# Turning q and k of two blocks in the two row halves of TensorE, in a kernel of gated attention and an FFN

## The chip, the cores and the metric

The kernel runs on one core of a Trainium2 chip. The metric is the device time of that core in microseconds (us). A core has a matrix engine (TensorE, in profiles PE, with its weight loads listed apart as PEld), a vector engine (DVE), a scalar engine (ACT), GpSimd (POOL), and a queue (SP) from which this kernel issues its DMA transfers. Matmuls read SBUF and write PSUM, which has eight banks of 512 fp32 values in each of 128 partitions; DVE and ACT read the results there.

## What is computed

A gated linear recurrence over 768 steps, for 4 batches of 8 heads with 48 channels, and a feed-forward network (FFN) on its output:

```python
# q, k, v, alpha: (4, 8, 768, 48); alpha in [0.8, 1.0)
for t in range(S):
    state = alpha[:, :, t, :, None] * state + np.einsum('bhd,bhe->bhde', k[:, :, t], v[:, :, t])
    y[:, :, t] = np.einsum('bhd,bhde->bhe', q[:, :, t], state)
# (B, H, S, D) -> (B*S, H*D) = (3072, 384)
x = y.transpose(0, 2, 1, 3).reshape(B * S, H * D)
h = np.maximum(x @ w_in, 0.0)      # w_in (384, 2048)
out = h * h @ w_out                # w_out (2048, 384)
```

The kernel computes the recurrence in 24 blocks of 128 tokens (6 stretches of each of 4 batches), with all 8 heads of a block in one tile. With b the running product of alpha within the block (the exponential of a cumulative sum of logarithms), q is multiplied by b and k by 1/b. The scores of a block are then a matmul of k and q, masked to the causal part, and the state enters and leaves a block through small matmuls. Matmuls contract over partitions, so for the scores q and k, which are loaded with a token in each partition, have to be turned: channels into partitions. TensorE does this with transposes against an identity matrix.

## The kernel before

Blocks come in groups of four (GB = 4). Group 0 runs first, in a fixed order; its FFN follows, with the attention of group 1 woven between its matmuls, and so on: while group g goes through its FFN, group g + 1 goes through its attention, in pairs of blocks. `PLAN` gives the places of a pair's steps in units of the FFN work; 20 blocks in 10 pairs are handled in this way. The heads are padded to 64 channels in the tiles of q and k, so that 128 columns hold two heads (a pair p of heads; NP = 4).

```python
    def kept(name, n, shape):
        return [consts.tile(shape, FP32, name=f"{name}{i}") for i in range(n)]
    s_t = [p2.tile([128, NP, 64], FP32, tag="s", name="s", bufs=B + 2) for _ in range(B)]
    for t in s_t:
        nc.gpsimd.memset(t, 0.0)
    NV = 4
    tiles = {
        "a": kept("a_in", 2, [128, H * D]), "q": kept("q_in", 2, [128, H, 64]),
        "k": kept("k_in", 3, [128, H, 64]), "v": kept("v_in", NV, [128, H * D]),
    }
    # ... cut ...
    def load(n, xs="aqkv"):
        c, b = divmod(n, B)
        for x in xs:
            t = tile_of(x, n)
            t = t[:, :, 0:D] if x in "qk" else t.rearrange("a (h d) -> a h d", h=H)
            src = srcs[x][b, :, c * C : (c + 1) * C, :].rearrange("h s d -> s h d")
            step = H // 2 if n == 0 and x in "ak" else H
            for h in range(0, H, step):
                nc.sync.dma_start(out=t[:, h : h + step], in_=src[:, h : h + step])
    # ... cut ...
    for n, xs in ((0, "akq"), (1, "aqk")):
        load(n, xs)
    # ... cut ...
    def warm(_):
        nc.tensor.matmul(
            out=ps_att.tile([128, NP, 64], FP32, tag="att", name="warm"),
            lhsT=s_t[0].rearrange("a p d -> a (p d)")[:, 0:128], rhs=s_t[0], start=True, stop=True,
        )
    # ... cut ...
    def bank(n, name, shape=(NP, C)):
        if n < GB and name in ("sc", "y"):
            return ps_ffn.tile([128, *shape], FP32, tag="f", name=name)
        return ps_att.tile([128, *shape], FP32, tag="att", name=name)
    # ... cut ...
    def ln(n):
        la = blk[n]["la"] = tile_of("a", n)
        for c in parts(n):
            nc.scalar.activation(out=la[:, c], in_=la[:, c], func=AF.Ln)
    def parts(n):
        return [slice(0, H * D)] if n else [slice(i * DM // 2, (i + 1) * DM // 2) for i in range(2)]
    def cs(n):
        ps = blk[n]["cs"] = bank(n, "cs")
        la = blk[n].pop("la")
        for c in parts(n):
            nc.tensor.matmul(
                out=ps.rearrange("a p t -> a (p t)")[:, c], lhsT=causal, rhs=la[:, c],
                start=True, stop=True, skip_group_check=True,
            )
    def sums_of_logs(n):
        return blk[n]["cs"].rearrange("a p t -> a (p t)")[:, 0 : H * D]
    def eb(n):
        b = blk[n]["b"] = p2.tile([128, H * D], FP32, tag="b", name="b")
        nc.scalar.activation(out=b, in_=sums_of_logs(n), func=AF.Exp)
    def ei(n):
        inv = blk[n]["inv"] = p2.tile([128, H * D], FP32, tag="inv", name="inv")
        for c in parts(n):
            nc.scalar.activation(
                out=inv[:, c], in_=sums_of_logs(n)[:, c], func=AF.Exp, scale=-1.0
            )
    def scaled(x, n, factor):
        for c in parts(n) if x == "k" else [slice(0, H * D)]:
            t = tile_of(x, n)[:, c.start // D : c.stop // D, 0:D]
            nc.vector.tensor_tensor(
                out=t, in0=t, in1=factor[:, c].rearrange("a (h d) -> a h d", d=D), op=ALU.mult
            )
    # ... cut ...
    def turned(x, n):
        rows = tile_of(x, n).rearrange("a h d -> a (h d)")
        ps = blk[n][f"{x}T"] = bank(n, f"{x}T")
        for p in range(NP):
            nc.tensor.transpose(
                out=ps[:, p, :], in_=rows[:, 128 * p : 128 * (p + 1)], identity=ident
            )
    def qT(n):
        turned("q", n)
    def kT(n):
        turned("k", n)
    VECTOR = ("k1", "k2", )
    def copied(x, n):
        t = blk[n][f"{x}s"] = work(f"{x}s", 2 if x == "k" else 4)
        copy = nc.vector.tensor_copy if f"{x}{n}" in VECTOR else nc.scalar.copy
        copy(out=t, in_=blk[n].pop(f"{x}T"))
    def qc(n):
        copied("q", n)
    def kc(n):
        copied("k", n)
    # ... cut ...
    HALF = [slice(0, 64), slice(64, C)]
    two = {}
    def scores(n):
        ps = two[n] = [bank(n, "sckv", (2, NP, 64)) for _ in range(2)]
        ks, qs = blk[n]["ks"], blk[n]["qs"]
        for p in range(NP):
            for h in range(2):
                for e in range(2):
                    rows = slice(64 * e, 64 * e + D)
                    nc.tensor.matmul(
                        out=ps[e][HALF[h], 0, p, :], lhsT=ks[rows, p, HALF[h]],
                        rhs=qs[rows, p, HALF[h]], start=True, stop=True, skip_group_check=True,
                    )
    # ... cut ...
    def state_sums(n):
        ps = two[n]
        for p in range(NP):
            for e in range(2):
                first = (2 * p + e) * D - G * e
                for h in range(1 if n // B == NCH - 1 else 2):
                    nc.tensor.matmul(
                        out=ps[h][64 * e : 64 * (e + 1), 1, p, :],
                        lhsT=tile_of("k", n)[HALF[h], 2 * p + e, :],
                        rhs=tiles["v"][n % NV][HALF[h], first : first + 64],
                        start=True, stop=True, skip_group_check=True,
                    )
    # ... cut ...
    def ga(a, n):
        if n is not None:
            for f in (scores, state_sums, masked, sums_copied):
                f(n)
        if a is not None:
            product = y_begin(a)
            for h in range(2):
                for m, p, e in heads(a):
                    rows = slice(64 * e, 64 * e + D)
                    s = blk[m]["u" if h else "s"]
                    product(m, p, e, s[rows, p, 0 : D + G * e], blk[m]["qs"][rows, p, HALF[h]], HALF[h])
            for m, p, e in heads(a):
                end = inner(product, m, p, e, e)
    # ... cut: the rest of ga, and gb, which does the same for block n + 1, then ev(a) copies y out of PSUM ...
    first = """
        warm0 ln0 load0v cs0 ei0 eb0 mk0 mq0 load2a load2q load2k bl0 ln1 kT0 qT0 kc0
        load1v qc0 cs1 load3a sc0 load3k eb1 mq1 bl1 qT1 load2v ei1 mk1 weights0 kT1 kc1
        ...
    """
    PLAN = (
        (0, "ln0"),
        (0.5, "ln1"),
        (2.0, "cs0 eb0 ei0"),
        (3.0, "cs1 eb1 ei1"),
        (3.5, "mk0"),
        (4.0, "bl0"),
        (4.5, "mq0 mk1 bl1"),
        (5.0, "mq1"),
        (6.5, "qT0 qc0 qT1 qc1 kT1 br1"),
        (7.5, "kc1"),
        (8.0, "kT0 kc0 br0"),
        (9.5, "ga"),
        (10.5, "gb"),
    )
```

`turned` is called four times for a pair of blocks (q and k of each): each call does four full 128x128 transposes into one PSUM bank, and `copied` brings the bank to SBUF with one copy. `ps_att` has four banks, which all steps of the attention share in turn; `ps_ffn` has the other four. The scores and state sums use quarters of the array (64 rows by 64 columns), with the two halves of the tokens in different quarters. `parts` and the step in `load` treat the first block by halves of its heads.

Of the kernel before, what the change touches and what calls it, by code (L numbers as in the profile page):

```python
# [10 lines left out]
AF = mybir.ActivationFunctionType  # L11
ALU = mybir.AluOpType
# [3 lines left out]
GB = 4  # L16
# [7 lines left out]
def kernel(  # L24
# [25 lines left out]
    nc = tc.nc  # L50
    B, H, S, D = q.shape
    C = 128
    NCH = S // C
    NP = H // 2
    NBLK = B * NCH
    DM, DF = moe_w_in.shape
# [37 lines left out]
    def flat(t):  # L94
        return t.rearrange("a x y -> a (x y)")
# [4 lines left out]
    for x, n, i in (("q", 2, 6), ("q", 3, 7), ("k", 3, 5)):  # L100
        t = lent[x, n] = flat(w_out[i])[:, 0 : 64 * H].rearrange("a (h d) -> a h d", h=H)
        nc.gpsimd.memset(t[:, :, D:64], 0.0)

    def tile_of(x, n):
        return lent.get((x, n), tiles[x][n % len(tiles[x])])


    srcs = {"a": alpha, "q": q, "k": k, "v": v}

    def load(n, xs="aqkv"):  # L110
        c, b = divmod(n, B)
        for x in xs:
            t = tile_of(x, n)
            t = t[:, :, 0:D] if x in "qk" else t.rearrange("a (h d) -> a h d", h=H)
            src = srcs[x][b, :, c * C : (c + 1) * C, :].rearrange("h s d -> s h d")
            step = H // 2 if n == 0 and x in "ak" else H
            for h in range(0, H, step):
                nc.sync.dma_start(out=t[:, h : h + step], in_=src[:, h : h + step])

    raws = {}  # L120

# [56 lines left out]
        )  # L178
        nc.vector.tensor_tensor(out=w, in0=w, in1=power.bitcast(FP32), op=ALU.mult)

    for n, xs in ((0, "akq"), (1, "aqk")):
        load(n, xs)
    to_load = list(range(2 * NW))
    stage = [3]
# [18 lines left out]
    ident = consts.tile([128, 128], FP32, name="ident")  # L203
    make_identity(nc, ident)
    causal = consts.tile([128, C], FP32, name="causal")
    make_upper_triangular(nc, causal, 1.0, diag=True)
    halves_mask = consts.tile([128, C // 2], FP32, name="halves_mask")
    for i in range(2):
        rows = slice(64 * i, 64 * (i + 1))
# [20 lines left out]
    blk = [{} for _ in range(NBLK)]  # L230
    xT = {}
# [7 lines that stand above are left out]
    def work(name, bufs=1):  # L239
        return p2.tile([128, NP, C], FP32, tag=name, name=name, bufs=bufs)  # L240

    def ln(n):
        la = blk[n]["la"] = tile_of("a", n)
        for c in parts(n):
            nc.scalar.activation(out=la[:, c], in_=la[:, c], func=AF.Ln)

    def parts(n):

        return [slice(0, H * D)] if n else [slice(i * DM // 2, (i + 1) * DM // 2) for i in range(2)]

    def cs(n):

        ps = blk[n]["cs"] = bank(n, "cs")
        la = blk[n].pop("la")
        for c in parts(n):
            nc.tensor.matmul(  # L256
                out=ps.rearrange("a p t -> a (p t)")[:, c], lhsT=causal, rhs=la[:, c],
                start=True, stop=True, skip_group_check=True,
            )

    def sums_of_logs(n):
        return blk[n]["cs"].rearrange("a p t -> a (p t)")[:, 0 : H * D]
# [4 lines left out]

    def ei(n):
        inv = blk[n]["inv"] = p2.tile([128, H * D], FP32, tag="inv", name="inv")
        for c in parts(n):  # L270
            nc.scalar.activation(
                out=inv[:, c], in_=sums_of_logs(n)[:, c], func=AF.Exp, scale=-1.0
            )

    def scaled(x, n, factor):
        for c in parts(n) if x == "k" else [slice(0, H * D)]:
            t = tile_of(x, n)[:, c.start // D : c.stop // D, 0:D]
            nc.vector.tensor_tensor(
                out=t, in0=t, in1=factor[:, c].rearrange("a (h d) -> a h d", d=D), op=ALU.mult
            )  # L280

    def mq(n):
        scaled("q", n, blk[n]["b"])
# [32 lines left out]
# [3 lines that stand above are left out]
        copy(out=t, in_=blk[n].pop(f"{x}T"))  # L319

    def qc(n):
        copied("q", n)

    def kc(n):
        copied("k", n)


    def zeros(n):
# [77 lines left out]
    HALF = [slice(0, 64), slice(64, C)]  # L406
# [57 lines left out]
    def dep(later, earlier):  # L464
        tc.add_manual_dep(
            later.ins, earlier.ins.name,
            mybir.DependencyInfo(mybir.DependencyClass.Sync, mybir.DependencyReason.DATA),
            reason="rows of TensorE change banks",
        )

    def inner(product, m, p, e, h):
        head = 2 * p + e
        return product(
            m, p, e, tiles["v"][m % NV][HALF[h], head * D - G * e : (head + 1) * D],
            am_h(m)[HALF[h], e, m % 2, p, :], HALF[h],
        )

    def heads(a):
        return [(m, p, e) for m in (a, a + 1) for p in range(NP) for e in range(2)]
# [23 lines left out]
    def gb(a, n):  # L503

        if a is not None:
            product, passed = two.pop("y")
            for i, (m, p, e) in enumerate(heads(a)):
                begin = inner(product, m, p, e, 1 - e)
                if i == 0:
                    dep(begin, passed)  # L510
        if n is not None:
            for f in (scores, state_sums, masked, sums_copied, next_state):
                f(n + 1)
        if a is not None:
            ev(a)
            for m in (a, a + 1):
                blk[m].clear()

    def ev(n):
        g, t = divmod(n, GB)  # L520
        if t == 0:
            xT[g] = x_pool.tile([128, KM, GB * C], FP32, tag="xT", name="xT")
        x = xT[g].rearrange("a k (t c) -> a k t c", c=C)

        for p in range(NP):
            for e, f, end in ((1, 2 * p * D + 32, 2 * (p + 1) * D), (0, 2 * p * D, (2 * p + 1) * D)):
                copy = nc.vector.tensor_copy if n in SHARED and e else nc.scalar.copy
                r = 64 * (e ^ p % 2)
                while f < end:
                    kk, to = divmod(f, 128)  # L530
                    m = min(end - f, *(RUN[i % 128] for i in (r, to)))
                    copy(  # L532
                        out=x[to : to + m, kk, t : t + 2],
                        in_=blk[n]["y"][e][r : r + m, :, p // 2],
                    )
                    r, f = r + m, f + m
        blk[n].pop("y")
# [21 lines left out]
    hid, acc, ws, xs, sums = {}, {}, {}, {}, {}  # L559
# [208 lines left out]


    stages = [(ln, cs, eb, ei, mq, mk, bl, br), (qT, qc, kT, kc), (sc, am), (kv, y, ev, st)]  # L770
    steps = {f.__name__: f for stage in stages for f in stage}
    steps["load"] = load
# [16 lines left out]
    for word in first.split():  # L789
        f = max((x for x in steps if word.startswith(x)), key=len)  # L790
# [12 lines left out]
        (4.0, "bl0"),  # L803
        (4.5, "mq0 mk1 bl1"),
        (5.0, "mq1"),
        (6.5, "qT0 qc0 qT1 qc1 kT1 br1"),
        (7.5, "kc1"),
        (8.0, "kT0 kc0 br0"),
        (9.5, "ga"),
        (10.5, "gb"),  # L810
    )
# [1 line left out]
    def attention(pairs, scale):  # L813


        out = []
        for t, n0, after, *last in pairs:
            for at, fs in PLAN:
                for f in fs.split():
                    w = t + at * scale  # L820
                    if f in ("ga", "gb"):
                        given = n0 - 2 if after else None, None if last or n0 >= NBLK else n0
                        out.append((w, {"ga": ga, "gb": gb}[f], given))
                    if last:
                        continue
                    if f == "ga" and n0 + 3 < NBLK:
                        out.append((w, load, (n0 + 3, "k")))
                    elif f == "gb":
                        for m, x in ((n0 + 2, "v"), (n0 + 3, "v"), (n0 + 4, "k")):
                            if m < NBLK:  # L830
                                out.append((w, load, (m, x)))
                    elif f != "ga" and n0 < NBLK:
                        n = n0 + int(f[-1])
                        out.append((w, steps[f[:-1]], (n,)))
                        x = {"cs": "a", "qT": "q"}.get(f[:-1])
                        if x and n + 2 < NBLK:
                            out.append((w, load, (n + 2, x)))
        return sorted(out, key=lambda x: x[0])

    def weave(units, events):  # L840
# [16 lines left out]
    events += [(0, load, (GB + 1,)), (1.0, load, (GB + 2, "k"))]  # L857
    events += [(47 + 2 * r, sum_w_in, (r,)) for r in range(NR2 - 1)]
    events += attention([(0, GB, False), (18.0, GB + 2, True), (27.5, GB + 4, True, True)], 2.35)
    events += [(53, sum_x, (1,)), (54, sum_w_in, (NR2 - 1,))]  # L860
    weave(units, sorted(events, key=lambda x: x[0]))
    for g in range(1, NG):
# [8 lines left out]
        if g + 1 < NG:  # L871
            n = GB * (g + 1) + 2
# [35 lines left out]
```

## Time and profile before

| | |
|---|---|
| time, median of 3 runs | 572.44 us (572.15 to 572.45) |
| span of the profiled execution | 570.2 us, mean granted TensorE clock 0.999 |
| TensorE busy from 0 to 42 us | 34.78 us |
| transposes (L303) from 42 us to the end | 160, of 272 to 273 ns each as a rule |
| copies of turned q and k on ACT | 46 of 128x512, 586 to 588 ns on average |
| first FFN matmul at the full rate (128x512) | starts at 38.87 us |

In the lines quoted below, a group reads: source line, engine, operation, output<-inputs by tile name, shape and type, count | busy us, mean ns of one | idle time of the engine just before them and what ended it. A shape such as 48*64 before the operand says how many rows and columns of the array are used. A line of the timeline reads: start in us, length in us, engine, source line, operation, tiles, shape, number of instructions merged into it, and the idle time before. Matmuls with fp32 operands appear as two records each, transposes as one. L303 are the transposes of q and k, L319 their copies out of PSUM, L345 the scores of group 0, L416 and L442 the scores and state sums of the later groups, L615 and L653 the first FFN matmul, L690 and L724 the second.

### The profile page before, as it was taken

To read this page: it belongs to the slowest core of one execution; us is meant where nothing else is said; L and a number is where in the kernel's file an instruction comes from. 1 tells how busy PE (TensorE), PEld (TensorE's weight loads), DVE (VectorE), ACT (ScalarE), POOL (GpSimd) and SP (SyncE) were. 2 spreads that over 40 slices of the span, in tenths; PEclk is the share of its full clock that TensorE was granted. 3 is DMA by queue.
4 is the path that set the end of the run, shared out by engine and by line. 5 is a ranking of instruction groups with operands and counts; after the bars stand their busy time and mean duration, and the time that the engine had idled before them with its cause. 6 is when DMAs were issued, how large, how long until landed. Compare 5 with 4: busy or idle time off the path is not lost.

```text
span 570.2 us, 12181 instructions
## 1 busy us (share of the span) xinstructions
PE 558.4 (98%) x5148; PEld 477.6 (84%) x5148; DVE 327.2 (57%) x656; ACT 222.6 (39%) x495; POOL 5.8 (1%) x28
## 2 busy tenths in 40 slices
PE   8889999999999999999999999999999999999997
PEld 6654556668889899888999988999988999988996
DVE  4888679585874644565462566462466551466440
ACT  4569955443334344333243333433333340333200
POOL 2010000000000000000000000000000000000000
PEclk9999999999999999999999999999999999999999
DMA  9978667401003545000333200333300000100001
GB/s 160 245 180 212 159 159 231 114 1 55 2 0 57 111 87 113 29 1 4 62 75 73 72 2 0 57 59 60 94 2 0 1 2 2 55 1 2 0 1 55
DMA packets 117117, 37.01 MB, mean 65 GB/s; under 512 B 108852, under 2 KB 111944, under 8 KB 117064
## 3 DMA queue, kind: packets, MB, share of 16 engines
q1 hardware_dynamic: 117064, 36.25, 28.3%
q8 instruction: 40, 0.66, 0.5%
q14 instruction: 13, 0.11, 0.1%
HBM read 31.49 MB, written 4.75 MB: 64 GB/s over the span
## 4 chain that ended last, share of the span: by engine, by line
PE 95%; DVE 2%; DMA 1%; issue 1%; SPq 0%; ACT 0%; POOL 0%; DVEq 0%; POOLq 0%
PE h L653 33%; PE o L724 32%; PE o L690 7%; PE h L615 7%; PE y L392 4%; PE cs L256 3%; PE sckv L416 2%; PE qT L303 2%; PE sckv L442 2%; PE kT L303 2%; DMA raw<-in_moe_w_in_dram 1%; PE warm L221 1%; PE sc L345 0%; DVE xT L532 0%; PE kv L362 0%
## 5 line engine op out<-in xcount | busy, mean ns | idle before, releaser
L653 PE MATMUL h<-xT,w_in 128*128 128x256 f32 x480 | 124.0, 379 | 0.0
L653 PEld LDWEIGHTS h<-xT,w_in 128*128 128x128 f32 x480 | 91.1, 190 | 12.4
L724 PE MATMUL o<-w_out,hid 128*128 128x192 f32 x480 | 82.5, 326 | 0.0
L724 PEld LDWEIGHTS o<-w_out,hid 128*128 128x128 f32 x480 | 79.1, 190 | 4.0
L532 ACT COPY xT<-y 32x256 f32<-32x256 f32 (+2 forms) x132 | 46.3, 365 | 57.8 <-PE y L392 54.2
L666 DVE TENSOR_TENSOR hid<-h,u 128x256 f32<-128x256 f32 x120 | 50.9, 424 | 28.8 <-PE h L653 25.0
L671 ACT ACTIVATE hid<-hid 128x256 f32<-128x256 f32 x40 | 16.7, 417 | 114.6 <-DVE hid L666 114.6
L666 DVE TENSOR_TENSOR u<-h,u 128x256 f32<-128x256 f32 x80 | 33.9, 423 | 34.8 <-PE h L653 22.4
L653 PE MATMUL h<-s3x,ws 128*128 128x256 f32 x160 | 47.6, 379 | 0.0
L426 DVE COPY_PREDICATED am<-halves_mask,sckv 128x256 f32<-128x256 uint32 x40 | 15.5, 442 | 55.0 <-PE sckv L442 55.0
L615 PE MATMUL h<-xT,w_in 128*128 128x512 f32 (+1 forms) x108 | 43.5, 549 | 3.3 <-ACT xT L532 1.8
L690 PE MATMUL o<-w_out,hid 128*128 128x384 f32 x128 | 42.8, 489 | 0.0
L724 PE MATMUL o<-t,s 128*128 128x192 f32 x240 | 41.8, 327 | 0.0
L653 PE MATMUL h<-s3x,w_in 128*128 128x256 f32 x160 | 41.1, 379 | 0.0
L724 PEld LDWEIGHTS o<-t,s 128*128 128x128 f32 x240 | 39.1, 190 | 0.7
L615 PEld LDWEIGHTS h<-xT,w_in 128*128 128x128 f32 x108 | 20.0, 190 | 22.9 <-issue 15.8
L690 PEld LDWEIGHTS o<-w_out,hid 128*128 128x128 f32 x128 | 23.8, 190 | 15.9 <-DVE s L461 0.2
L653 PEld LDWEIGHTS h<-s3x,ws 128*128 128x128 f32 x160 | 30.4, 190 | 4.1
L653 PEld LDWEIGHTS h<-s3x,w_in 128*128 128x128 f32 x160 | 30.4, 190 | 4.1
L724 PE MATMUL o<-t,hid 128*128 128x192 f32 x160 | 28.3, 328 | 0.0
L673 DVE SCALAR_TENSOR_TENSOR hid<-hid 128x512 f32<-128x512 f32 x40 | 27.3, 682 | 0.0
L758 DVE TENSOR_TENSOR osb<-o,us 128x384 f32<-128x384 f32 x10 | 5.6, 558 | 37.1 <-PE o L724 37.1
(114 smaller groups left out, 758.4 us busy)
## 6 DMA issues: line engine op xcount, KB each, us to landing
raw<-in_moe_w_in_dram SPq DMA_DIRECT2D x8, 768.0 KB
raw<-in_moe_w_out_dram SPq DMA_DIRECT2D x8, 768.0 KB, 7.2
v_in<-in_v_dram SPq DMA_DIRECT2D x24, 192.0 KB, 4.3
out_dram<-osb SPq DMA_DIRECT2D x24, 192.0 KB, 2.0
q_in<-in_q_dram SPq DMA_DIRECT2D x22, 192.0 KB, 3.4
k_in<-in_k_dram SPq DMA_DIRECT2D x22, 192.0 KB, 4.4
a_in<-in_alpha_dram SPq DMA_DIRECT2D x21, 192.0 KB, 2.7
last<-row SPq DMA_DIRECT2D x40, 0.8 KB, 3.7
```

The costliest lines, as they stand in the source:

```text
L256: nc.tensor.matmul(out=ps.rearrange("a p t -> a (p t)")[:, c], lhsT=causal, rhs=la[:, c], start=True, stop=True, skip_group_check=True,)
L303: nc.tensor.transpose(out=ps[:, p, :], in_=rows[:, 128 * p : 128 * (p + 1)], identity=ident)
L392: ins = nc.tensor.matmul(out=ys[e][64 * half : 64 * half + D + G * e, m % 2, p // 2, t], lhsT=lhsT, rhs=rhs, start=(half, e) not in seen, ...
L426: nc.vector.copy_predicated(out=am_h(n)[:, e, n % 2], data=ps[e][:, 0], mask=halves_mask.bitcast(U32).unsqueeze(1).to_broadcast([128, NP, ...
L532: copy(out=x[to : to + m, kk, t : t + 2], in_=blk[n]["y"][e][r : r + m, :, p // 2],)
L615: nc.tensor.matmul(out=ps, lhsT=w[:, kk, c0 : c0 + 128], rhs=xT[g][:, kk, cols], start=(kk == 0), stop=(kk == KM - 1),)
L653: nc.tensor.matmul(out=ps, lhsT=a, rhs=b, start=(step.isupper() and i == 0), stop=(i == len(pairs) - 1), skip_group_check=True,)
L666: nc.vector.tensor_tensor(out=o, in0=ps, in1=z, op=ALU.add)
L671: nc.scalar.activation(out=h1[:, HT : 2 * HT], in_=h1[:, HT : 2 * HT], func=AF.Relu)
L673: nc.vector.scalar_tensor_tensor(out=h2, in0=h2, scalar=0.0, in1=h2, op0=ALU.max, op1=ALU.mult)
L690: nc.tensor.matmul(out=acc[t][:, 0:DM], lhsT=hid[i][:, j, t * C : (t + 1) * C], rhs=w_out[i][:, j, :], start=(i == 0 and j == 0), stop=(i ...
L724: nc.tensor.matmul(out=acc[k][:, t, :], lhsT=lhs[:, j, t * C : (t + 1) * C], rhs=rhs[:, j, :], start=(first and r + j + t == 0), stop=(r = ...
```

## The change

From the second group on, one function `turn` does all transposes of a pair of blocks in one stretch. A transpose takes 64 tokens (the upper or the lower 64 rows of the array) and 128 columns; the two halves of the tokens alternate, so that the two row halves of TensorE can work at the same time, and each half has a PSUM bank of its own: four banks for a pair. Each bank holds k and q of one half of a block's tokens. The copies out of PSUM therefore take two instructions of 128x256 for each tensor. Group 0 keeps the full transposes. In the same change, the first block's alpha and k are loaded and worked on whole, and its loads go out in the order alpha, q, k.

```diff
--- before.py
+++ after.py
@@ -111,11 +111,10 @@
         c, b = divmod(n, B)
         for x in xs:
             t = tile_of(x, n)
-            t = t[:, :, 0:D] if x in "qk" else t.rearrange("a (h d) -> a h d", h=H)
-            src = srcs[x][b, :, c * C : (c + 1) * C, :].rearrange("h s d -> s h d")
-            step = H // 2 if n == 0 and x in "ak" else H
-            for h in range(0, H, step):
-                nc.sync.dma_start(out=t[:, h : h + step], in_=src[:, h : h + step])
+            nc.sync.dma_start(
+                out=t[:, :, 0:D] if x in "qk" else t.rearrange("a (h d) -> a h d", h=H),
+                in_=srcs[x][b, :, c * C : (c + 1) * C, :].rearrange("h s d -> s h d"),
+            )
 
     raws = {}
 
@@ -178,7 +177,7 @@
         )
         nc.vector.tensor_tensor(out=w, in0=w, in1=power.bitcast(FP32), op=ALU.mult)
 
-    for n, xs in ((0, "akq"), (1, "aqk")):
+    for n, xs in ((0, "aqk"), (1, "aqk")):
         load(n, xs)
     to_load = list(range(2 * NW))
     stage = [3]
@@ -241,22 +240,15 @@
 
     def ln(n):
         la = blk[n]["la"] = tile_of("a", n)
-        for c in parts(n):
-            nc.scalar.activation(out=la[:, c], in_=la[:, c], func=AF.Ln)
-
-    def parts(n):
-
-        return [slice(0, H * D)] if n else [slice(i * DM // 2, (i + 1) * DM // 2) for i in range(2)]
+        nc.scalar.activation(out=la, in_=la, func=AF.Ln)
 
     def cs(n):
 
         ps = blk[n]["cs"] = bank(n, "cs")
-        la = blk[n].pop("la")
-        for c in parts(n):
-            nc.tensor.matmul(
-                out=ps.rearrange("a p t -> a (p t)")[:, c], lhsT=causal, rhs=la[:, c],
-                start=True, stop=True, skip_group_check=True,
-            )
+        nc.tensor.matmul(
+            out=ps.rearrange("a p t -> a (p t)")[:, 0 : H * D], lhsT=causal,
+            rhs=blk[n].pop("la"), start=True, stop=True,
+        )
 
     def sums_of_logs(n):
         return blk[n]["cs"].rearrange("a p t -> a (p t)")[:, 0 : H * D]
@@ -267,17 +259,13 @@
 
     def ei(n):
         inv = blk[n]["inv"] = p2.tile([128, H * D], FP32, tag="inv", name="inv")
-        for c in parts(n):
-            nc.scalar.activation(
-                out=inv[:, c], in_=sums_of_logs(n)[:, c], func=AF.Exp, scale=-1.0
-            )
+        nc.scalar.activation(out=inv, in_=sums_of_logs(n), func=AF.Exp, scale=-1.0)
 
     def scaled(x, n, factor):
-        for c in parts(n) if x == "k" else [slice(0, H * D)]:
-            t = tile_of(x, n)[:, c.start // D : c.stop // D, 0:D]
-            nc.vector.tensor_tensor(
-                out=t, in0=t, in1=factor[:, c].rearrange("a (h d) -> a h d", d=D), op=ALU.mult
-            )
+        t = tile_of(x, n)[:, :, 0:D]
+        nc.vector.tensor_tensor(
+            out=t, in0=t, in1=factor.rearrange("a (h d) -> a h d", h=H), op=ALU.mult
+        )
 
     def mq(n):
         scaled("q", n, blk[n]["b"])
@@ -319,10 +307,10 @@
         copy(out=t, in_=blk[n].pop(f"{x}T"))
 
     def qc(n):
-        copied("q", n)
+        (copied if n < GB else turned_copied)("q", n)
 
     def kc(n):
-        copied("k", n)
+        (copied if n < GB else turned_copied)("k", n)
 
 
     def zeros(n):
@@ -515,6 +503,24 @@
             ev(a)
             for m in (a, a + 1):
                 blk[m].clear()
+
+    def turn(n):
+
+        for m in (n, n + 1):
+            ps = blk[m]["T"] = [bank(m, "T", (2, NP, 64)) for _ in range(2)]
+            for i, x in enumerate("kq"):
+                rows = tile_of(x, m).rearrange("a h d -> a (h d)")
+                for p in range(NP):
+                    for h in range(2):
+                        nc.tensor.transpose(
+                            out=ps[h][:, i, p, :], in_=rows[HALF[h], 128 * p : 128 * (p + 1)],
+                            identity=ident[HALF[h], HALF[h]],
+                        )
+
+    def turned_copied(x, n):
+        t = blk[n][f"{x}s"] = work(f"{x}s", 2 if x == "k" else 4)
+        for h in range(2):
+            nc.scalar.copy(out=t[:, :, HALF[h]], in_=blk[n]["T"][h][:, "kq".index(x)])
 
     def ev(n):
         g, t = divmod(n, GB)
@@ -803,9 +809,8 @@
         (4.0, "bl0"),
         (4.5, "mq0 mk1 bl1"),
         (5.0, "mq1"),
-        (6.5, "qT0 qc0 qT1 qc1 kT1 br1"),
-        (7.5, "kc1"),
-        (8.0, "kT0 kc0 br0"),
+        (6.5, "turn br1"),
+        (7.0, "kc0 qc0 kc1 qc1 br0"),
         (9.5, "ga"),
         (10.5, "gb"),
     )
@@ -829,12 +834,16 @@
                         for m, x in ((n0 + 2, "v"), (n0 + 3, "v"), (n0 + 4, "k")):
                             if m < NBLK:
                                 out.append((w, load, (m, x)))
+                    elif f == "turn":
+                        if n0 < NBLK:
+                            out.append((w, turn, (n0,)))
+                            for m in range(n0 + 2, min(n0 + 4, NBLK)):
+                                out.append((w, load, (m, "q")))
                     elif f != "ga" and n0 < NBLK:
                         n = n0 + int(f[-1])
                         out.append((w, steps[f[:-1]], (n,)))
-                        x = {"cs": "a", "qT": "q"}.get(f[:-1])
-                        if x and n + 2 < NBLK:
-                            out.append((w, load, (n + 2, x)))
+                        if f[:-1] == "cs" and n + 2 < NBLK:
+                            out.append((w, load, (n + 2, "a")))
         return sorted(out, key=lambda x: x[0])
 
     def weave(units, events):
```

## The prediction

> **What bounds the kernel now.** I began with the page: the span, the busy shares of the engines, and the shares of the chain that ended last.
>
> ```profile
> span 570.2 us, 12181 instructions
> PE 558.4 (98%) x5148; PEld 477.6 (84%) x5148; DVE 327.2 (57%) x656; ACT 222.6 (39%) x495; POOL 5.8 (1%) x28
> PE 95%; DVE 2%; DMA 1%; issue 1%; SPq 0%; ACT 0%; POOL 0%; DVEq 0%; POOLq 0%
> ```
>
> TensorE (PE) is busy for 98% of the span and carries 95% of the chain. A busy share is an average, so I asked for busy times by stretch:
>
> ```profile
> core 0: us, PE busy (x) PEld busy (x) DVE busy (x) ACT busy (x) POOL busy (x), PEclk, DMA share, GB/s
> 0.00:42.00 42.00, 34.78 (x248) 26.16 (x249) 30.48 (x56) 22.91 (x47) 5.76 (x28) 1.00 0.96 196
> 42.00:100.00 58.00, 58.00 (x297) 30.98 (x296) 46.45 (x72) 42.53 (x69) 0.00 (x0) 1.00 0.73 189
> 100.00:180.00 80.00, 80.00 (x696) 63.23 (x695) 54.46 (x118) 30.99 (x73) 0.00 (x0) 1.00 0.14 36
> 180.00:230.00 50.00, 49.58 (x878) 45.94 (x877) 27.15 (x62) 20.95 (x50) 0.00 (x0) 1.00 0.52 100
> ```
>
> There are two regimes. In the first 42 us TensorE idles 7 us and the DMA engines are 96% busy: this is where group 0's attention waits for loads and for chains of small steps. From 42 us on TensorE is busy all the time (49.58 of 50 even in the stretch with most attention work). So time that the change takes off TensorE after 42 us comes off the end, one for one, as long as no new wait opens; a change to the first block moves only the latency chain of the first regime.
>
> Next, the groups by line and form that the change touches: the transposes, the matmuls that already use only part of the array, and the copies out of PSUM.
>
> ```profile
> L303 PE MATMUL kT<-ident,k_in 128*128 128x128 f32 x92 | 13.9, 273 | 0.9 <-DVE k_in L278 0.9
> L303 PE MATMUL qT<-ident,q_in 128*128 128x128 f32 x88 | 11.9, 274 | 0.6 <-DVE q_in L278 0.5
> L345 PE MATMUL sc<-qs,ks 48*128 48x128 f32 x64 | 4.6, 285 | 0.0
> L319 ACT COPY qs<-qT 128x512 f32<-128x512 f32 x24 | 13.1, 586 | 24.1 <-PE qT L303 24.0
> L658 ACT COPY u<-h 128x256 f32<-128x256 f32 x40 | 14.4, 359 | 16.3 <-PE h L653 16.3
> ```
>
> A matmul's duration includes its way through the pipeline, so its cost is the step from one start to the next. That I read from the timeline, where a stretch of n equal instructions lasts (n-1) steps and one duration:
>
> ```profile
> 13.05 1.16 PE L345 MATMUL sc<-qs,ks 48*128 48x128 f32 x16
> ...
> 17.41 0.60 PE L303 MATMUL kT<-ident,k_in 128*128 128x128 f32 x4
> ...
> 73.49 0.65 PE L442 MATMUL sckv<-v_in,k_in 64*64 64x64 f32 x32
> 74.07 0.91 PE L256 MATMUL cs<-a_in,causal 128*128 128x384 f32 x2
> ...
> 200.85 1.46 PE L724 MATMUL o<-w_out,hid 128*128 128x192 f32 x8
> 202.24 0.69 PE L416 MATMUL sckv<-qs,ks 48*64 48x64 f32 x32
> ```
>
> A full transpose with 128 moving columns: (0.60-0.272)/3 = 109 ns. The group-0 scores (rows 0-47 and 64-111 in turn, all 128 array columns, 128 moving columns): (1.16-0.272)/15 = 59 ns, so the two row halves run side by side. The small scores, 64x64 parts of the array with 64 columns: (0.69-0.218)/31 = 15 ns, so four parts run side by side and TensorE can start a load and a matmul every 15 ns.
>
> Changing the shape of the array costs something. Into the small shape: the last of the eight L724 matmuls starts 7 x 162 ns after 200.85, at 201.98, and the first L416 follows 0.26 us later instead of 0.162: about 93 ns extra (the unrounded records give 256 against 163 ns). Out of it: the last L442 starts at 73.49+0.65-0.219 = 73.92 and the full-array matmul at 74.07, 148 ns against a step of 14: about 134 ns extra. Together 0.227 us per visit. The full transposes of before pay none of this: their records follow one another and the FFN matmuls without a gap.
>
> **What the skill says.** "TensorE: Matmul & The Clock Gate", Part 3 (packing small matmuls): matmuls in different row groups of the array run concurrently, and a weight load overlaps running matmuls where its row group differs. The trace agrees for ordinary matmuls (59 ns in place of 109), but shows no transpose in half the rows. "TensorEngine Tiling (Array Packing)", Key Properties: changing the tiling mode drains the engine. The trace agrees, at 93+134 ns. The same page under Restrictions says that column tiling switches off the FP32 transpose mode; the new transposes use row halves and all the columns, so it should not apply, but it is the nearest thing to a warning. "PSUM — Partial Sum Buffer", the section on bank collisions: different row tiles may not write the same bank at once. That is why the new code has a bank for each half; the trace shows no instance of a clash.
>
> **The change part by part.** *Removed:* 20 blocks (24 less group 0's 4) x 8 full transposes = 160 (the trace counts 160 of L303 after 42 us), x 109 ns = 17.5 us of TensorE.
>
> *Added:* 20 x 2 tensors x 4 pairs x 2 halves = 320 transposes of 64 tokens x 128 columns, with 64 moving columns. Alone such a one should take half of 109, 54.5 ns, and two side by side 27.3 ns each. The scores in the same two-row shape reached 59 instead of 54.5 ns, 8% more, so I take 59/2 = 29.6 ns (an estimate): 320 x 29.6 = 9.5 us. The weight load must keep up too. For all 128 columns the transpose's load lasts 140 ns where an ordinary one lasts 190; the shorter one streams about 53 ns faster, so two loads in different halves should fit in the same step. Each turn is one visit to the new shape: 10 x 0.227 = 2.3 us. The sum is 17.5-9.5-2.3 = 5.7 us saved.
>
> *Copies:* each tensor now comes from two banks, so ScalarE (ACT) does 80 copies of 128x256 at 359 ns instead of 40 of 128x512 at 587: 28.7 against 23.5 us, 5 us more busy time on an engine at 39%. Eight follow in one row, some 2.9 us. In the compiled order the scores of the first block stand four FFN units (10 us) after the turn in the first pair, and three product units (3 x 8 x 0.163 = 3.9 us) after it in the later groups; the first block's four copies need about 1.5 us. So they should be hidden. The fullest ACT stretch (42 to 100 us, 42.5 of 58 us) can be late by some tenths. Allowance: +0.3 us.
>
> *First block unsplit:* ln0 ran as two halves, at 2.96 and 4.05 us, each on the landing of its half. Whole, it waits for the second landing (about 4.05) and takes 0.52: done by 4.6. The cumulative sum could not start before 4.67 anyway, because the warm-up matmuls hold TensorE until then. After it, inv takes 0.49 instead of 0.36 for its first half, and k's product 0.55 instead of half of it: kT moves from 7.06 to about 7.3 us, qT (next on DVE) from 7.86 to about 7.95. k now lands after q, by my estimate near 5.7 us, before inv is done at 6.7. Two fewer DMA issues let the later loads go out up to 1 us earlier, but DMA is 96% busy there, and DVE waits 0.70 us for the first w_in piece at 21.6 us, which absorbs small delays. Net: +0.1 us, within +-0.5.
>
> Total: -5.7+0.3+0.1 = -5.3 us, so 567.1; I say 567.0.
>
> **Rivals.** (1) *Transposes do not run side by side in the row halves.* Then 320 x 54.5 = 17.5 us, nothing saved, and the 2.3 us of shape changes come on top: 575. For it: no transpose in half rows in the trace, and the skill's restriction nearby. Against it: the shared loads and matmuls of sc. One in ten. (2) *They overlap in part* (a load that lasts longer than the 64 columns, or a start-to-start limit): at 40 ns, 12.8+2.3 us, a gain of 2.4: 570. (3) *A new wait takes the place.* All four PSUM banks of the attention pool are filled by one turn, and y needs the second pair's back; a late ACT would stop TensorE at the scores or at y. If each of ten turns lost 0.5 us, all but 0.7 us of the gain would be gone: 572. Against it: before, the only TensorE wait after 42 us in the list of waits is one of 0.3 us, for DVE's q. (4) *The start loses more*, if k lands late: +1 us, 568.
>
> **Range and chances.** The best case is perfect overlap (27.3 ns, 8.7 us), cheaper shape changes (1.5) and no loss: 7.3 us saved, 565. With partial overlap or late copies 570 to 571; rival 1 lies outside. Range 564.8 to 570.6. The 2% mark is 11.4 us; even free transposes with no shape change would save 17.5, and real ones at most 8.7, so faster by 2% has 1 in 100; slower by 2% needs stalls on top of rival 1: 2 in 100.
>
> **What would show it.** The new transposes at a step of 27 to 30 ns in one stretch of 32 of about 1.15 us (0.95 plus a pipeline time); 0.2 to 0.25 us of extra start gaps about each turn; FFN rows as before; no TensorE wait on ACT at the scores or y; the first FFN matmul at its time of before within 0.5 us. Steps of 54 ns would mean rival 1; idle before L416 or L392 rival 3.

## The result and the profile after

The changed kernel takes 568.81 us (median of three runs, 568.75 to 569.17) where the kernel before takes 572.44: a ratio of 0.994, with a 95% interval of 0.9917 to 0.9963. That is 3.6 us less, well inside the 2%. The prediction said 567.0, 5.4 us less: inside its range, but with a third of the gain missing. Where that third went is the subject of the experiments.

The page of the changed kernel has the same picture as before, with all spans a little shorter: the span, the busy shares and the chain by engine.

```profile
span 566.8 us, 12556 instructions
PE 554.1 (98%) x5306; PEld 471.1 (83%) x5306; DVE 327.0 (58%) x655; ACT 223.6 (39%) x533; POOL 5.8 (1%) x28
PE 95%; DVE 2%; DMA 1%; issue 1%; ACT 0%; SPq 0%; POOL 0%; POOLq 0%
```

TensorE has 158 more matmuls and is busy 4.3 us less. The groups by line and form show the new transposes and their copies (columns as before: count | busy us, mean ns | idle before, releaser):

```profile
L515 PE MATMUL T<-ident,k_in 64*128 64x64 f32 x160 | 8.9, 230 | 0.0
L515 PE MATMUL T<-ident,q_in 64*128 64x64 f32 x160 | 8.4, 224 | 0.0
L523 ACT COPY qs<-T 128x256 f32<-128x256 f32 x40 | 13.8, 422 | 0.0
L523 ACT COPY ks<-T 128x256 f32<-128x256 f32 x40 | 13.3, 397 | 23.6 <-PE T L515 23.6
```

320 transposes with 64 rows and all 128 columns of the array, and 80 copies, as counted in advance. The ACT copies wait for TensorE, never TensorE for them: in the list of waits after 42 us TensorE has one entry only, and it is another one.

```profile
PE y L380 <- issue: 1.3, 1, 1.3
```

One turn in the timeline of the changed kernel (start, length, then the instructions merged into the line):

```profile
177.69 1.63 PE L730 MATMUL o<-t,s 128*128 128x192 f32 x9
179.24 0.46 PE L515 MATMUL T<-ident,k_in 64*128 64x64 f32 x8
179.54 0.42 PE L515 MATMUL T<-ident,q_in 64*128 64x64 f32 x8
179.79 0.42 PE L515 MATMUL T<-ident,k_in 64*128 64x64 f32 x8
180.05 0.42 PE L515 MATMUL T<-ident,q_in 64*128 64x64 f32 x8
180.39 1.57 PE L730 MATMUL o<-t,s3x 128*128 128x192 f32 x8
```

Three things are to be read here. From the first to the last start of the 32 transposes pass 995 ns by the unrounded records (995 to 1001 in the turns without a wait). They start in twos, 3 or 4 ns apart, and the next two some 60 ns later; only the second two come 107 or 108 ns after the first. Eight FFN matmuls after the turn take 1.57 us, where eight of the same kind otherwise take 1.46 (a line of the kernel before, below): 104 ns more, all of it between the first and the second matmul.

TensorE's longest stop is elsewhere. In the stage that starts near 279 us, in the middle of y, TensorE stands still:

```profile
280.80 0.57 PE L380 MATMUL y<-am,v_in 64*48 64x64 f32 x23
282.63 0.34 PE L380 MATMUL y<-am,v_in 64*48 64x64 f32 x8 [1.26 <-issue]
```

"issue" says that no semaphore and no engine released it. Start to start the stop is 1.48 us, in a stretch whose normal step is 15 ns. Two smaller ones of 314 and 355 ns (at 220 and 310 us) don't reach the list of waits. Before, there was one such stop, of 327 ns.

### The profile page after: what moved, and what is told of

Read it like the earlier page. It is cut to its first block, busy times and chain, and to the rows that moved or that the text cites. A ratio compares the mean times of both kernels' runs of the same rounds, so it can differ in the third digit from the quotient of the medians.

```text
span 566.8 us, 12556 instructions
## 1 busy us (share of the span) xinstructions
PE 554.1 (98%) x5306; PEld 471.1 (83%) x5306; DVE 327.0 (58%) x655; ACT 223.6 (39%) x533; POOL 5.8 (1%) x28
## 4 chain that ended last, share of the span: by engine, by line
PE 95%; DVE 2%; DMA 1%; issue 1%; ACT 0%; SPq 0%; POOL 0%; POOLq 0%
PE h L659 34%; PE o L730 33%; PE o L696 7%; PE h L621 7%; PE y L380 4%; PE cs L248 3%; PE T L515 2%; PE sckv L404 2%; PE sckv L430 2%; DMA raw<-in_moe_w_in_dram 1%; PE warm L220 1%; PE sc L333 0%; DVE xT L538 0%; PE kv L350 0%; PE qT L291 0%
```

## The experiments

### The two parts apart

In the first pair of profiles the first FFN matmul at the full rate starts at 38.46 us where it started at 38.87, so part of the gain seemed to come from the start, against the prediction's +0.1 us. Two kernels take one part of the change each: `e1_turn_only` has the turn and keeps the first block's halves, `e2_unsplit_only` has the unsplit first block and the full transposes of before.

```diff
# e1_turn_only: the changed kernel, except
-    for n, xs in ((0, "aqk"), (1, "aqk")):
+    for n, xs in ((0, "akq"), (1, "aqk")):
+            step = H // 2 if n == 0 and x in "ak" else H     # in load; ln, cs, ei, scaled over parts(n)
# e2_unsplit_only: the changed kernel, except
-        (6.5, "turn br1"),
-        (7.0, "kc0 qc0 kc1 qc1 br0"),
+        (6.5, "qT0 qc0 qT1 qc1 kT1 br1"),
+        (7.5, "kc1"),
+        (8.0, "kT0 kc0 br0"),
```

> The turn alone; the first block keeps its halves. Theory A: the start and the turn are two separate gains, and in the changed kernel 0.4 us of the 3.6 come from the start (first 128x512 FFN matmul at 38.46 in place of 38.87 us). Then this run takes 569.2 us, its first 128x512 FFN matmul stands at 38.9 us, and after it every turn costs what it costs in the changed kernel (1.00 us from its first to its last start). Rival: the 0.4 us at the start are chance or come with the turn; then 568.8 us and 38.5. On the stop of 1.48 us inside y of the changed kernel (281 us): TensorE's instruction stream moves here by only a few instructions, so the stop should be there again, whatever its cause.

> The unsplit first block alone, with the full transposes of before. Theory A: 572.0 us, 0.4 us less than before, with the first 128x512 FFN matmul at 38.5 us. Rival of the prediction (the start loses): 572.5 to 573.5 us.

Measured: turn only 570.49 us (ratio to before 0.9964, interval 0.9946 to 0.9982), first full-rate FFN matmul at 38.68 us, turns of 994 to 1000 ns without a wait, and the stop of 1.47 us at 281.51. Unsplit only 573.3 us (1.0007, 0.9999 to 1.0015), first full-rate FFN matmul at 39.51. (All times here count from the first instruction of each timeline; some in the expectations below count from another zero and differ by up to 0.4 us.) The second is the opposite of what I expected: the same code that reached 38.46 in the changed kernel reached 39.51 here. The timelines show why, first the changed kernel, then this one:

```profile
7.42 0.63 PE L291 MATMUL kT<-ident,k_in 128*128 128x128 f32 x4 [1.26 <-DVE k_in L266]
8.35 0.81 PE L248 MATMUL cs<-a_in,causal 128*128 128x384 f32 x2
...
7.42 1.09 PE L291 MATMUL kT<-ident,k_in 128*128 128x128 f32 x4 [1.26 <-DVE k_in L266]
9.15 1.49 PE L248 MATMUL cs<-a_in,causal 128*128 128x384 f32 x2
```

kT starts at the same time, but from there until about 10.6 us TensorE needs about twice as long for the same instructions, although the granted clock reads 1.00 in both. The landing of block 1's loads is not the cause: the logarithm of its alpha starts at 7.05 us here and at 6.96 in the changed kernel. The changed kernel itself, run again:

> The changed kernel again, for the same chip as the runs beside it. Both theories on the stops: 568.8 us, the stop of 1.48 us at the same matmul. On the start (the kernel with only the unsplit first block reached its first 128x512 FFN matmul at 39.66 us, this one at 38.41 with the same code up to there): if that is the landing of the loads of block 1, it can be 38.4 or up to 39.7 here; if it is the code, 38.4.

It took 569.31 us (0.9957, 0.994 to 0.9973) with that matmul at 38.71 and the stop of 1.48 us in its place. To settle the start, turn only and the whole change ran side by side in five rounds, with the same two kernel texts:

> Turn alone, first block in halves, side by side with the whole change on one chip. So far the first 128x512 FFN matmul stood at 38.84 and 38.87 us in two profiles with the halves and between 38.2 and 39.7 us in six without. Theory S (the unsplit start is worth nothing that can be measured): the two medians within 0.5 us of each other. Rival (the 0.4 us of the first pair of profiles are real): this one 0.4 to 0.5 us slower than the whole change.

> The whole change, for comparison with the turn alone and with the shifted stream. Theory S: within 0.5 us of the turn alone. Stop of 1.48 us at the same matmul of y in the stage at 281 us.

569.06 us (0.9952, 0.9938 to 0.9965) and 569.21 us (0.9947, 0.9935 to 0.996): no difference. Over all profiles the matmul stands at 38.53, 38.68 and 38.87 us with halves, and at 38.28 to 39.51 without (in the shifted kernels below, the first half of the same matmul). The four profiles later than 39 us each have a stretch in which TensorE ran at about half pace: two as shown above, and two shortly before the matmul, where the granted clock fell to 0.54 and 0.50 between 36 and 38.3 us. The first block's part is worth nothing that these runs can measure; whether it makes such stretches more likely stays open with three profiles against ten.

### Do the two row halves work at the same time?

`e3_halves_in_turn` keeps the 320 transposes but does four of one half, then four of the other.

```diff
-                for p in range(NP):
-                    for h in range(2):
+                for h in range(2):
+                    for p in range(NP):
```

> Same 320 transposes, but four of the upper half, then four of the lower half, instead of alternating. Theory A (the gain is row halves working side by side): within a half the step becomes 54 to 62 ns and only the step at a change of half is short, so a turn takes about 1.46 us from first to last start instead of 1.00, and the kernel 573 to 574 us: the gain over before is gone. Rival (a half-size transpose costs about 31 ns by itself, in whatever order): 1.00 us a turn and 568.8 us.

It took 569.14 us (0.9936, 0.9916 to 0.9956), and a turn took 1.04 us from first to last start. The timeline of this kernel:

```profile
179.32 0.47 PE L515 MATMUL T<-ident,k_in 64*128 64x64 f32 x8
179.62 0.47 PE L515 MATMUL T<-ident,q_in 64*128 64x64 f32 x8
179.87 0.47 PE L515 MATMUL T<-ident,k_in 64*128 64x64 f32 x8
180.13 0.46 PE L515 MATMUL T<-ident,q_in 64*128 64x64 f32 x8
```

So my theory, as I had put it, missed: the order in the program hardly matters. Two readings were left: TensorE pairs the halves by itself, or one half needs no partner for this pace. `e5_one_half` decides. All its transposes use the upper half, so the results for the lower half's tokens are made from the upper half's: it computes something else with the same instructions.

```diff
-                            out=ps[h][:, i, p, :], in_=rows[HALF[h], 128 * p : 128 * (p + 1)],
-                            identity=ident[HALF[h], HALF[h]],
+                            out=ps[h][:, i, p, :], in_=rows[HALF[0], 128 * p : 128 * (p + 1)],
+                            identity=ident[HALF[0], HALF[0]],
```

> The last experiment (four transposes of one half, then four of the other) left the pace at 31 to 34 ns, so either TensorE pairs the halves whatever their order in the program, or a half-size transpose needs no partner. Here all 320 transposes use the upper row half: the lower half's results are made from the upper half's tokens, so the output is another one, the count and shape of the instructions the same. Theory A (two halves at work at once): 54 to 62 ns a step, 1.7 to 1.9 us a turn from first to last start in place of 1.00, 7 to 9 us more than the changed kernel in the span: 574 to 576 us. Theory B (31 ns each by itself): 1.0 us a turn and the span of the changed kernel, 566.8 us.

578.52 us (1.0111, 1.0091 to 1.0131), slower than before. A turn in its timeline:

```profile
181.12 0.71 PE L515 MATMUL T<-ident,k_in 64*128 64x64 f32 x8
181.67 0.67 PE L515 MATMUL T<-ident,q_in 64*128 64x64 f32 x8
182.18 0.67 PE L515 MATMUL T<-ident,k_in 64*128 64x64 f32 x8
182.69 0.67 PE L515 MATMUL T<-ident,q_in 64*128 64x64 f32 x8
```

The groups of eight now follow at 0.51 to 0.55 us instead of 0.25 to 0.30; every step after the first (112 ns) is 60 to 65 ns and a turn is 2.00 us. The span is 576.3 us against 566.8, and ten turns at 1.0 us more account for it. So one half-size transpose costs 62 to 65 ns, and only the partner in the other half brings that to 31. The previous run then means that TensorE started transposes of the second half ahead of earlier ones of the first: in program order, four of one half need at least 3 x 62 ns and eight such groups 1.5 us, and they took 1.04. Which half a record belongs to is not in the trace, but the records hold one more sign. Each half has its own bank, and the load that must wait for the second half's bank carries that wait. In this program's instruction stream that load is the fifth of its block; in the trace it starts second, in all 15 blocks (of 20) that have such a wait, 13 ns after the first load in the first turn.

### What a visit to another shape of the array costs

`e4_two_visits` splits each turn: one block, an FFN unit, the other block.

```diff
-        (6.5, "turn br1"),
-        (7.0, "kc0 qc0 kc1 qc1 br0"),
+        (6.5, "turn br1"),                  # block n0 only, and the load of n0 + 2's q
+        (7.0, "kc0 qc0"),
+        (7.5, "turn2 kc1 qc1 br0"),         # block n0 + 1, and the load of n0 + 3's q
```

> The turn of a pair in two visits, one block each, with an FFN unit between: 10 more visits of the small array shape, no other work. Theory A: a visit costs 93 ns on the way in, 121 to 133 ns at the first full matmul after it and another 104 ns at the second, 0.32 to 0.33 us in all, and the first pair of transposes some 50 ns more: +3.7 us, so 572.5 us, and one more start gap of 163+104 ns after each visit. Rival (the prediction's sum, 0.227 us a visit, the 104 ns gaps belonging to something else): +2.3 to 2.8 us, 571.1 to 571.6, with no more gaps of 104 ns than before.

574.31 us (1.0024, 1.0013 to 1.0035), slower than before, and 1.8 us more than I expected. Its timeline:

```profile
180.79 0.65 PE L736 MATMUL o<-t,s 128*128 128x192 f32 x3
181.37 0.46 PE L521 MATMUL T<-ident,k_in 64*128 64x64 f32 x8
181.67 0.42 PE L521 MATMUL T<-ident,q_in 64*128 64x64 f32 x8
182.02 1.57 PE L736 MATMUL o<-t,s3x 128*128 128x192 f32 x8
183.51 0.46 PE L521 MATMUL T<-ident,k_in 64*128 64x64 f32 x8
```

After each visit eight full matmuls take 1.57 us. Counted over the trace, gaps of 104 ns more than the step number 24 in the kernel before, 34 with the turn and 44 here (after 42 us): exactly one for each return from a small shape to the full array. A visit to the small shape costs 93 ns ahead of it (257 against 163 in the records), 154 ns from the last small start to the first full one, where a step of the stretch would be 30, and 104 ns at the second full one: 0.32 us. It was there to be seen in the kernel before, at the visits of the scores, where I had read only the first two:

```profile
188.57 1.46 PE L724 MATMUL o<-t,s 128*128 128x192 f32 x8
...
190.47 0.65 PE L442 MATMUL sckv<-v_in,k_in 64*64 64x64 f32 x32
191.05 1.57 PE L724 MATMUL o<-t,s3x 128*128 128x192 f32 x8
```

The first L724 line follows on a full matmul, cs, and takes 1.46 us; the second follows on a visit and takes 1.57. Ten more visits thus cost 3.4 us here (1.686 us for two in place of 1.350 for one, times ten). The rest of this run's loss against the changed kernel (its span is 571.7, 4.9 more) is in stops: it has four, of 1.56, 0.41, 1.65 and 0.27 us, together 3.9 in place of 2.1. So the visits alone don't make it slower than before: two visits of 0.843 us a pair still cost less than the 1.747 us of full transposes.

### The stops

The stops fall on no wait and no particular step of the program, but they have a common place. Take TensorE's instructions in the order of their starts: loads, matmuls, and also its semaphore and drain instructions, which the trace holds though the page leaves them out of the busy counts. Then each stop comes after the same number modulo 256.

```
kernel         stop at us  length us  instruction  modulo 256
before         287.35      0.33       5313         193
after          220.11      0.31       4289         193
after          281.15      1.48       5313         193
after          309.82      0.36       6337         193
two visits     102.01      1.56       1473         193
two visits     284.50      1.65       5313         193
```

The thirteen profiles have 27 stops of 0.25 us or more between small matmuls after 42 us, and all 27 come after instruction 193 modulo 256. The queue named q8 in the profile carries instructions: 42 packets and 0.69 MB, 16 KB each, in the changed kernel, with 10713 instructions on TensorE, 255 for each packet. "Runtime: NRT & Kernel Launch" in the Trainium skill, under instruction fetch mechanics, says that instructions are brought in blocks of 16 KiB, 256 of them, while the block before runs, and that this is mostly hidden. The trace agrees with the size, but at these 27 places the fetch isn't hidden. Scores, state sums and y use parts of the array of 64x64 or less with a step of 15 ns, a load and a matmul each, so that the last 256 instructions before the long stop went in 1.89 us. A packet of q8 had begun 1.2 us before this stop and took 1.08 us. In all 27 stops TensorE went on 2.2 to 3.1 us after the latest packet had begun.

If the stops are waits for instructions, they must move when the stream is shifted. `e6_shift168` and `e7_shift84` let 14 or 7 of the FFN units of group 0 (group 1 in the expectation's words) do each of their three matmuls as two of 256 columns instead of one of 512: four more instructions for each, 12 a unit, at the same TensorE time (the step is 216 ns for 256 columns and 429 for 512).

```diff
-        for kk in range(KM):
-            nc.tensor.matmul(out=ps, lhsT=..., rhs=xT[g][:, kk, cols], ...)
+        step = HT if n > HT and j < 16 else n          # e7_shift84: j < 9
+        for c in range(0, n, step):
+            for kk in range(KM):
+                nc.tensor.matmul(out=ps[:, c : c + step], lhsT=..., rhs=xT[g][:, kk, ... c : c + step], ...)
```

> The stops inside scores, state sums and y of the changed kernel (0.31 us at 220, 1.48 at 281, 0.36 at 310) all come at the same place of TensorE's instruction stream modulo 256 instructions, which are the 16 KB that one transfer of the instruction queue brings. Here group 1's 14 FFN units load their weights twice for 256 columns each instead of once for 512: 168 more instructions ahead of the attention that stops, at the same TensorE time (216 ns for 256 columns against 429 for 512). Theory F (the stops are waits for instructions): the stop at the 24th matmul of y<-am in the stage at 281 us is gone, stops come 168 instructions earlier in the stream, where only one stretch from boundary to boundary is as short as 1.9 us (near 217 us); 1 to 1.5 us faster than the changed kernel if that one is on time. Rival G (the stop belongs to that spot of the program: a bank or a semaphore): the stop stays at the same matmul, and the time is that of the changed kernel.

> As the run before, with seven units split: 84 more instructions. Theory F: no stop at the 24th matmul of y<-am in the stage at 281 us; stops, if any, at other places, the same modulo 256 counted with the added instructions: the three short stretches (1.85 to 2.0 us from boundary to boundary) end near 203, 372 and 397 us. Rival G: the stop at 281 us stays.

With 168 more: 568.34 us (0.9928, 0.991 to 0.9946), one stop of 0.51 us, at 284 us, after instruction 5569 (193 modulo 256). With 84 more: 568.29 us (0.9932, 0.9911 to 0.9954), one stop of 0.41 us at 201.81 us, after instruction 3521 (193). The stretch that stood still runs through in the timeline of the second:

```profile
280.88 0.68 PE L380 MATMUL y<-am,v_in 64*48 64x64 f32 x31
281.49 1.57 PE L733 MATMUL o<-t,s 128*128 128x192 f32 x8
```

The long stop is gone in both, and those that remain keep the position modulo 256, with the added instructions counted. A bank or a semaphore at that spot of the program would have kept the stop at its matmul. The one near 202 us was expected there; those expected near 372 and 397 us didn't come, nor the one near 217 us in the first, and the one at 284 us there wasn't foreseen. So it is shown that the stops belong to the blocks of 256 instructions, but not a rule for which block arrives late. The kernel with 84 more ran again beside the whole change:

> The changed kernel with 84 more instructions ahead of the later groups. Theory F (stops are waits for instructions): one stop of about 0.4 us near 202 us in place of 1.5 to 2.1 us of stops, so 1.0 to 1.5 us faster than the whole change beside it and the fastest of all; rival: the same time.

568.14 us (0.9934, 0.9922 to 0.9946; runs from 567.40 to 568.76) against 569.21 (568.36 to 569.51): 1.1 us less by the medians, the fastest here, though the ranges overlap. In that profile there were two stops where I had expected one, 0.58 us at 203 us and 0.33 us at 221 us, and the long one was absent again.

## Why the prediction was right, and where it was off

The time lies in the range, and the mechanism was right: transposes in the two row halves side by side take TensorE time away, and TensorE's time comes off the end. By its steps:

*Removed.* 1.747 us of full transposes a pair (1201+109 and 327+109 ns in the records), 17.5 us in all: as put.

*"59/2 = 29.6 ns".* The turn takes 0.998 us between first and last start, not 31 x 29.6 = 0.918. Halving the columns did not halve the step: in the unrounded records the twos of the scores (128 columns) follow at 112 ns, those of the turn (64 columns) at 63, some 7 ns more than half. Besides, the second two come some 48 ns late. The 59 ns of the scores hid both, since it is an average over a stretch whose own second two come 102 ns late. Mis-sized by 0.08 us a turn, 0.8 us.

*"Together 0.227 us per visit".* This is the main error in the sum: a visit costs 0.32 us. I took the end of the visit for the first full matmul and missed the 104 ns at the second: 0.9 us in ten visits.

With these, a pair's turn costs 0.093+0.998+0.154+0.104 = 1.349 us in place of 1.747: 4.0 us for ten pairs, where I had put 5.7.

*No new wait, and "allowance: +0.3 us" for ACT.* No TensorE wait on ACT after 42 us; rival 3 as written did not come about, with copies of 397 to 422 ns each, longer than the 359 I took. A gain that I hadn't counted: the waits for DVE's q in the second pair of group 2 cost 0.80 us before by the starts (the list of waits counts 0.3 of it), 0.26 now, since k goes first and the last q is needed later.

*What I had no step for: the supply of instructions.* The stops rose from 0.3 to 2.1 us (0.31+1.48+0.36, less the normal steps). The change adds 341 instructions to TensorE's stream, which moves the ends of the blocks of 256 against the fast stretches, and one of them fell badly. This 1.8 us is the largest single piece of the missing gain, and would have been another with another count of instructions.

*The start.* kT began at 7.42 us (I said 7.3), qT at 7.89 (7.95), and the first w_in piece went out 0.6 us earlier (14.36 for 14.97). The net of +0.1 within 0.5 was too narrow only in that single profiles of one kernel differ by more: 38.46, 38.71 and 39.15 us in the three of the changed kernel.

Sum for the two profiles: turns -4.0, q wait -0.5, stops +1.8, start -0.4 (chance, by the repeats): -3.1 us. The unrounded spans differ by 3.3; 0.2 us isn't accounted for. Without the two gains that I hadn't counted, 0.9 us together, the time would have been about 569.7, still inside the range.

Of the rivals, the first (no overlap) was tried directly in the kernel with one half only: had the hardware behaved so, the change would have lost some 6 us. The second, overlap in part, is what the extra 0.08 us a turn amounts to.

## What to carry to other kernels

Before moving work to a smaller shape of the array, price the visit from a trace of the same kernel, by the start of the second full matmul after it and not only of the first: here 0.32 us, so that ten visits ate 3.2 of the 7.2 us that the smaller transposes saved, and twenty would have left 0.6 us of gain; with stops of 3.9 us on top the kernel was slower than before. Where many small matmuls follow at a step of 15 ns, TensorE can run out of instructions, and a change anywhere ahead moves those stops; look for stops that the profile puts down to issue before blaming the change, and try a shift of the stream.

## What the runs showed that I had not expected

Transposes for one row half, placed together in the program, still shared the array with those of the other half (33.7 ns a step, 1.044/31, against 64.7 with one half alone): the interleaved order that the change took care to write is worth 0.05 us a turn. A half-size transpose alone costs 62 to 65 ns where the full one costs 109. And TensorE, with no wait on data, stood still for up to 1.65 us at a time, always after the same instruction of 256.
